# First expert's outputs of the last 1536 tokens by seven block products, and routing rounds spaced wider

## The chip, the core and the metric

One core of one Trainium2 chip. The metric is the device time of one execution in microseconds (us). Engines are named as in the profile: PE does the matmuls, PEld their weight loads, DVE, ACT and POOL are the vector, scalar and GpSimd engines, SP issues DMAs. PSUM has eight banks of 128 x 512 f32; matmuls write there, DVE and ACT read from there, and POOL works in SBUF.

## The reference

An attention with sorted key and value blocks gives x (3072 tokens of 512). What matters here is what follows: a routing matrix from a softmax balanced in eight rounds, and eight experts, each a two-layer network on all tokens, summed with the routing weights.

```
logits = x @ w_gate                       # 3072 x 8
P = np.exp(logits - logits.max())
for _ in range(8):
    P /= P.sum(1, keepdims=True) + 1e-09  # a row step
    P /= P.sum(0, keepdims=True) + 1e-09  # a column step
    P *= N / E
for e in range(8):
    h = np.maximum(x @ w1[e], 0.0)        # 512 -> 1024, the hidden layer
    out += P[:, e:e+1] * (h @ w2[e])      # 1024 -> 512, the output layer
```

## The kernel before

**Tiles.** Tokens are in 24 tiles of 128. xtT holds x transposed (four blocks of 128 features), hT a piece of the hidden layer, transposed, osbl the output sum (acc(t) is the part for tile t), glog the logits and later the routing weights, 24 x 8 per partition in f32.

**Stages.** Up to 106 us the four batches (768 tokens each) go through attention; the first expert's hidden and output layers for batches 0 and 1 are woven in. From 106.7 us on comes the part that changes: a loop of 56 slots (lines 867 to 881). In each slot the first expert does one step for batch 2 or 3 (last_two, line 837): a hidden step (hidden0, line 393) is four matmuls of 384 tokens and a relu on ACT; an output step (output0, line 402) is four matmuls of 512 columns, half of a tile's eight, and after two such steps the tile is copied from PSUM to osbl on ACT (keep, and keep_scaled for batch 3, which multiplies by the routing weight).

**Routing.** balance (line 642) is a generator whose 19 steps are dealt out to named slots. Three find the maximum and exponentiate; then each of eight rounds has a row step (five DVE instructions on glog, lines 668 to 672) and a column step (one matmul with ones on PE that sums over partitions, line 675, then three DVE instructions, 676 to 679). PE's part is kept in program order in all rounds, DVE's in the first five. Rounds end at slot 39.

**Other work in the loop.** From slot 27 on each slot also does a step of the second expert's hidden layer (hidden, line 688). Hidden and output layers of experts 1 to 7 use seven products of half blocks in place of eight (Strassen's scheme in Winograd's form). hidden makes four blocks of 128 x 512 in seven steps of two matmuls each; ACT takes three products to SBUF (lines 717, 721, 726) and one by relu (739), DVE merges three with a custom instruction that adds and clips (712) and subtracts a fourth into h3 (740). It needs sums of x made ahead: sum_x (line 121), four subtractions of 128 x 1024 bf16 on DVE for each 1024 tokens, in slots listed in works. sum_w makes the sums of w1, sum_w2 (line 631) those of w2, eight subtractions on POOL. scale0 (823) multiplies tiles of the first expert by the routing weight on ACT, six of them in the loop, twelve later; gather (744) multiplies later experts' products by their weight and adds them to osbl on DVE.

**Output by seven products.** output7 (line 766) takes a pair of tiles and makes seven products of four matmuls of 256 columns in two PSUM tiles, u and x. u is summed on through five products and read in between, so a product must wait for the read of the one before it in u. The sums of h that it needs are made on POOL by sum_h (755), three instructions for a pair: hs has the sums, h3 the difference that DVE made.

**Who waits where.** Buffers: hT two, h3 two, hs three, the pool bk five PSUM banks (hidden steps and the routing's small matmuls), op three (outputs). Instructions wrapped in pin stay in program order on their engine; the others may be moved by the scheduler that builds the program. At slot 40 a copy on POOL of the finished weights (held, line 880) comes ahead of the second expert's sum_w2 (sums(8)), so that POOL starts this work when routing is done. After the loop, two more hidden steps, and then (line 885) the 21 thirds of experts 1 to 7, each with four pairs of outputs beside the hidden steps of the next third.

Of the kernel before, what the change touches and what calls it, by code (L numbers as in the profile page):

```python
# [13 lines left out]
F32 = mybir.dt.float32  # L14
BF16 = mybir.dt.bfloat16
AF = mybir.ActivationFunctionType
# [9 lines left out]
def kernel(  # L26
# [15 lines left out]
    NT = 24  # L42
# [72 lines left out]
    def acc(t, c=0, n=Dm):  # L115
        return osbl[t // 18][:, t % 18, c:c + n]
# [276 lines left out]
    def hidden0(c0, hTs, hbank, fbs=range(8)):  # L393
        for fb in fbs:
            hps = hbank()
            for kk in range(4):
                pin(nc.tensor.matmul(hps[:, 0:384], w1t[0][:, kk, fb * 128:(fb + 1) * 128],  # L397
                                     xtT[:, kk, c0:c0 + 384], start=(kk == 0), stop=(kk == 3)))
            nc.scalar.activation(out=hTs[:, fb, 0:384], in_=hps[:, 0:384], func=AF.Relu)
            yield  # L400

    def output0(c0, hTs, obank, done, tts=range(3)):
        for tt in tts:
            oacc = obank()
            for fb in range(8):
                pin(nc.tensor.matmul(oacc, hTs[:, fb, tt * 128:(tt + 1) * 128],  # L406
                                     w2t[0][:, fb, :], start=(fb == 0), stop=(fb == 7)))
                if fb == 3:
                    yield
            done(c0 // 128 + tt, oacc)  # L410
            yield
# [1 line left out]
    def keep(t, oacc):  # L413
        (nc.vector.tensor_copy if 6 <= t < 12 else nc.scalar.copy)(acc(t), oacc)

    def keep_scaled(t, oacc):
        nc.scalar.activation(out=acc(t), in_=oacc, func=AF.Copy,
                             scale=glog[:, t, 0:1])

    wct = {}  # L420

    def sum_w(e):
# [123 lines left out]
    with ExitStack() as c2:  # L546
# [61 lines left out]
        for _ in ex:  # L608
# [12 lines left out]
    op = ctx.enter_context(tc.tile_pool(name="op", bufs=3, space=bass.MemoryType.PSUM,  # L621
                                        reuse_waits="tile"))
    osbl[1] = osp.tile([128, 6, Dm], F32, name="osbl1")
    load_w2(1)

    def bank():
        return bk.tile([128, 512], F32, name="bk")

    w2s = {}

    def sum_w2(e):
        w2s[e] = (w2q.tile([128, 4, 4, Dm // 2], BF16, name="w2s") if e % 2 else
                  wcp.tile([128, 4, 4, Dm // 2], BF16, name="w2e"))
        for k in (0, 2):
            b11, b12 = (w2t[e][:, 4 + k:6 + k, d:d + 256] for d in (0, 256))
            b21, b22 = (w2t[e][:, k:k + 2, d:d + 256] for d in (0, 256))
            t1, t2, t3, t4 = (w2s[e][:, j, k:k + 2, :] for j in range(4))
            for a, b, c in ((b12, b11, t1), (b22, t1, t2), (b22, b12, t3), (b21, t2, t4)):
                pin(nc.gpsimd.tensor_tensor(out=c, in0=a, in1=b, op=ALU.subtract))
                yield  # L640
# [100 lines left out]
                                       op0=ALU.max, op1=ALU.subtract)  # L741
        yield

    def gather(e, t, c, ps):
        o = acc(t, c, ps.shape[-1])
        nc.vector.scalar_tensor_tensor(out=o, in0=ps, scalar=glog[:, t, e:e + 1], in1=o,  # L746
                                       op0=ALU.mult, op1=ALU.add)

# [3 lines left out]

    hs = {}

    def sum_h(i, hT, f0=0, f1=4, hold=lambda ins: ins):

        if f0 == 0:
            hs[i] = hsp.tile([128, 3, 4, 128], BF16, name="hs")
        s1, s2, s4 = (hs[i][:, j, f0:f1] for j in range(3))
        a11, a21, a12, a22 = (hT[:, f + f0:f + f1, t + 128 * i:t + 128 * i + 128]  # L760
                              for f in (4, 0) for t in (0, 512))
        for a, b, o, c in ((a21, a22, ALU.add, s1), (s1, a11, ALU.subtract, s2),
                           (a12, s2, ALU.subtract, s4)):
            hold(nc.gpsimd.tensor_tensor(out=c, in0=a, in1=b, op=o))  # L764

    def output7(e, p, i, hT):
        a, b = 8 * p + i, 8 * p + 4 + i
        ha, hb = slice(128 * i, 128 * i + 128), slice(512 + 128 * i, 640 + 128 * i)
        s1, s2, s4 = (hs[i][:, j] for j in range(3))
        s3 = h3[e, p][:, :, ha]  # L770
        t1, t2, t3, t4 = (w2s[e][:, j] for j in range(4))
        obank = lambda: op.tile([128, Dm], F32, name="oacc")
        last = e == E - 1 and p == 2
        u = (bank if last and i % 2 else obank)()[:, 0:256]
        x = (bank if last and i else obank)()
        x0, x1 = x[:, 0:256], x[:, 256:512]
        b11, b21, b22 = w2t[e][:, 4:8, 0:256], w2t[e][:, 0:4, 0:256], w2t[e][:, 0:4, 256:512]

        def add(ps, h, w, first):
            for fb in range(4):  # L780
                nc.tensor.matmul(ps, h[:, fb, :], w[:, fb, :], start=(first and fb == 0),  # L781
                                 stop=(fb == 3), skip_group_check=True)

        def upper():
            add(u, hT[:, 4:8, ha], b11, True)
            gather(e, a, 0, u)

        def lower():
            add(x0, hT[:, 0:4, ha], b21, True)

        for one in (lower, upper) if a == 0 and e == 1 else (upper, lower):
            one()
            yield
        add(u, s2, t2, False)
        gather(e, a, 256, u)
        yield
        add(x1, s1, t1, False)
        gather(e, b, 256, x1)
        yield
        add(u, s3, t3, False)  # L800
        gather(e, b, 256, u)
        yield
        add(x1, s4, b22, False)
        gather(e, a, 0, x)
        store(e, a)
        yield
        add(u, hT[:, 0:4, hb], t4, False)
        gather(e, b, 0, u)
        store(e, b)
        yield  # L810

# [18 lines left out]
    def sums(n):  # L830
        while n and queue:
            if next(queue[0], 0) is None:
                n -= 1
            else:
                queue.pop(0)

    def last_two():
        for bb, done in ((2, keep), (3, keep_scaled)):
            hT = htp.tile([128, 8, 1024], BF16, name="hT")
            halves = [(bb * S + c, hT[:, :, c:c + 384]) for c in (0, 384)]  # L840
            for c0, hTs in halves:
                yield from hidden0(c0, hTs, bank)
            for c0, hTs in halves:
                yield from output0(c0, hTs, lambda: op.tile([128, Dm], F32, name="oacc"), done)

    hTs, AHEAD = {}, 5

# [12 lines left out]
            next(old)  # L860
            yield

    tail0, chain, ahead = last_two(), balance(), hiddens()
    x1, x2 = sum_x(1), sum_x(2)
    works = {12: x0, 18: x1, 22: x1, 25: x1, 26: x1, 41: x2, 43: x2, 46: x2, 48: x2}
    scaled = {41: 0, 42: 4, 43: 1, 45: 5, 47: 2, 49: 6}
    for n in range(56):
        next(tail0)
        if n >= 27:
            next(ahead)  # L870
            if n == 50:
                sum_h(0, hTs[0], 0, 3)
        if n in works:
            next(works[n], 0)
        if n in scaled:
            scale0([scaled[n]])
        if n in (0, 2, 4, 6, 9, 11, 14, 16, 19, 21, 23, 25, 27, 29, 31, 33, 35, 37, 39):
            next(chain)
        if n == 40:
            pin(nc.gpsimd.tensor_copy(held, glog[0:96, NT - 1, 0:2]))  # L880
            sums(8)

    for _ in range(28 + AHEAD - 2 - 29):
        next(ahead)
    for n in range(1, 3 * (E - 1) + 1):
        e, p, hT = 1 + (n - 1) // 3, (n - 1) % 3, hTs[n - 1]
        d = 2 + n // 3
        fetch = n == 1 or n % 3 == 0 and d < E
        if fetch:
            load_w1(d)  # L890
            queue.append(sum_w(d))
        for i in range(4):
            if e == 1:
                scale0([t for t in (8 * p + i, 8 * p + 4 + i)
                        if t < 18 and t not in scaled.values()])
            end = n == 3 * (E - 1)
            hold = pin if end else lambda ins: ins
            if i == 0:
                sum_h(0, hT, 3, hold=hold)
            if i < 3 - end:  # L900
                sum_h(i + 1, hT, 3 if end and i == 0 else 0, hold=hold)
            elif i == 3 and not end:
                sum_h(0, hTs[n], 0, 3)
                if n == 3 * (E - 1) - 1:
                    sum_h(1, hTs[n], 0, 3)
            sums(1 + i // 2)
            for _ in (output8 if end and i == 3 else output7)(e, p, i, hT):
                next(ahead, 0)
        if fetch:
            load_w2(d)  # L910
            queue.append(sum_w2(d))
# [30 lines left out]
```

## Time and profile before

| | us |
|---|---|
| median of 3 runs | 667.71 (667.61 to 667.75) |
| the profiled execution | 667.97 |
| its span, first to last instruction | 666.2 |
| the loop of 56 slots and two hidden steps, on PE | 106.7 to 163.8 |
| DVE busy, 118 to 130 us | 9.69 of 12.00 |
| DVE busy, 130 to 140 us | 7.98 of 10.00 |
| POOL busy, 106.8 to 140 us | 0 |
| POOL busy, 140 to 150 us | 5.99 of 10.00 |
| ACT busy, 130 to 140 us | 7.56 of 10.00 |

PE's granted clock is 0.999 of full speed. Read the table as one stage: PE has work all the time (no gap worth a line), ACT and DVE are three quarters busy, POOL stands idle until the routing rounds are through and works after that. In a line of a timeline the first number is the start in us, the second the duration, then engine, line, operation, output <- inputs, shapes, and in brackets the idle time before it with what ended it. Durations of one engine's neighbours overlap a little; the distance between starts is what an instruction takes of its engine.

### The profile page before, as it was taken

The page shows a single profiled execution, that of the slowest core. Times are in us where ns is not written, and L with a number is a line of the kernel's source. Part 1 is how long each engine was busy: PE and PEld are TensorE (multiplying, and loading weights), DVE is VectorE, ACT ScalarE, POOL GpSimd, SP SyncE. Part 2 cuts the span into 40 slices and gives each one's busy share as a digit, 9 for nine tenths or more (in the row PEclk, how much of TensorE's full clock was granted, in tenths as well). Part 3 has the DMA queues.
Part 4 walks back from the last instruction along what each step waited for, and adds up shares of the span by engine and source line. Part 5 has one row for each costly group of instructions (what it writes and reads, how often), then busy time and mean ns, then how long its engine had stood idle before and what let it go on. Part 6 is the DMA issues. An engine that isn't in the chain of part 4 may idle for free.

```text
span 666.2 us, 13218 instructions
## 1 busy us (share of the span) xinstructions
PE 658.0 (99%) x5141; PEld 435.5 (65%) x5141; DVE 557.9 (84%) x1128; ACT 300.3 (45%) x535; POOL 471.0 (71%) x500
## 2 busy tenths in 40 slices
PE   7999999999999999999999999999999999999997
PEld 3766675554666666666666666666666666666666
DVE  6656876785888898998989898988998989898996
ACT  5775773476455443333334333433343334333430
POOL 4813353037897998898897999689886999646652
PEclk9999999999999999999999999999999999999999
DMA  9998964003041240033103040034003130001124
GB/s 188 172 220 143 150 110 64 1 1 63 1 64 16 49 64 1 0 64 44 21 1 64 1 64 2 1 63 64 1 1 65 16 50 1 1 0 62 68 95 159
DMA packets 33375, 36.96 MB, mean 55 GB/s; under 512 B 2112, under 2 KB 26400, under 8 KB 33312
## 3 DMA queue, kind: packets, MB, share of 16 engines
q0 software_dynamic: 26784, 27.03, 25.9%
q1 hardware_dynamic: 6416, 8.99, 4.3%
q8 instruction: 40, 0.66, 0.4%
q14 instruction: 23, 0.19, 0.1%
q10 hardware_dynamic: 112, 0.10, 0.1%
HBM read 52.45 MB, written 6.29 MB: 88 GB/s over the span
## 4 chain that ended last, share of the span: by engine, by line
PE 95%; DVE 2%; DMA 1%; ACT 0%; issue 0%; POOL 0%; ACTq 0%; DVEq 0%; POOLq 0%
PE bk L694 38%; PE oacc L781 38%; PE bk L397 3%; PE bank L406 3%; PE oacc L406 3%; PE bank L397 2%; PE bank L244 1%; PE pair L365 1%; PE bank L204 1%; PE bank L226 1%; PE bk L781 1%; PE bank L255 1%; DMA vsb<-vs 1%; PE bk L817 1%; DVE vs L283 0%; PE bank L190 0%
## 5 line engine op out<-in xcount | busy, mean ns | idle before, releaser
L746 DVE SCALAR_TENSOR_TENSOR osbl<-oacc,glog,osbl 128x256 f32<-128x256 f32 (+1 forms) x490 | 255.7, 524 | 27.9 <-PE oacc L781 18.2
L764 POOL TENSOR_TENSOR hs<-hT 128x512 bf16<-128x512 bf16 (+2 forms) x105 | 98.6, 951 | 72.3 <-DVE hT L712 72.2
L694 PE MATMUL bk<-xtT,w1e 128*128 128x512 bf16 x504 | 148.6, 379 | 0.0
L712 DVE CUSTOM_DVE_ANT_0 hT<-bk,p 128x512 bf16<-128x512 f32 x168 | 116.1, 691 | 26.7 <-PE bk L694 23.5
L781 PEld LDWEIGHTS <-hT 128*128 128x128 bf16 x996 | 97.4, 98 | 62.6 <-issue 0.2
L781 PEld LDWEIGHTS <-hs 128*128 128x128 bf16 x996 | 97.4, 98 | 61.2 <-issue 1.6
L781 PE MATMUL oacc<-w2e,hT 128*128 128x256 bf16 x796 | 119.7, 273 | 0.0
L717 ACT COPY p<-bk 128x512 f32<-128x512 f32 x84 | 49.3, 587 | 147.4 <-PE bk L694 147.0
L764 POOL TENSOR_TENSOR hs<-hs,hT 128x512 bf16<-128x512 bf16 (+2 forms) x105 | 99.6, 958 | 4.5 <-ACT hT L739 0.2
L764 POOL TENSOR_TENSOR hs<-hT,hs 128x512 bf16<-128x512 bf16 (+2 forms) x105 | 99.1, 952 | 4.7
L694 PE MATMUL bk<-xc,wc 128*128 128x512 bf16 x336 | 99.8, 379 | 0.0
L739 ACT ACTIVATE hT<-bk 128x512 bf16<-128x512 f32 x84 | 50.2, 597 | 96.1 <-PE bk L694 96.1
L781 PE MATMUL oacc<-w2e,hs 128*128 128x256 bf16 x612 | 91.8, 273 | 0.0
L694 PEld LDWEIGHTS <-w1e 128*128 128x128 bf16 x672 | 65.7, 98 | 12.1
L740 DVE SCALAR_TENSOR_TENSOR h<-bk,hT 128x512 bf16<-128x512 f32 x84 | 57.2, 681 | 3.9 <-ACT hT L739 3.9
L712 DVE CUSTOM_DVE_ANT_0 hT<-bk,u 128x512 bf16<-128x512 f32 x84 | 58.0, 690 | 2.5 <-PE bk L694 2.5
L721 ACT COPY u<-bk 128x512 f32<-128x512 f32 x84 | 49.2, 586 | 23.8 <-PE bk L694 23.2
L726 ACT COPY p<-bk 128x512 f32<-128x512 f32 x84 | 49.3, 587 | 23.4 <-PE bk L694 23.4
L694 PEld LDWEIGHTS <-wc 128*128 128x128 bf16 x504 | 49.3, 98 | 8.0 <-issue 0.2
L781 PE MATMUL oacc<-w2s,hs 128*128 128x256 bf16 x364 | 53.3, 272 | 0.0
L694 PE MATMUL bk<-xtT,wc 128*128 128x512 bf16 x168 | 50.0, 379 | 0.0
L694 PE MATMUL bk<-xc,w1e 128*128 128x512 bf16 x168 | 50.0, 379 | 0.0
(149 smaller groups left out, 791.4 us busy)
## 6 DMA issues: line engine op xcount, KB each, us to landing
w1e<-in_moe_w_dram POOLq DMA_DIRECT2D x7, 1024.0 KB, 8.1
w2e<-in_moe_w_dram POOLq DMA_DIRECT2D x7, 1024.0 KB, 8.9
out_dram<-osbl SPq DMA_DIRECT2D x23, 256.0 KB, 2.0
kvq<-in_v_dram POOLq DMA_DIRECT2D x3, 768.0 KB, 10.6
kvq<-in_k_dram POOLq DMA_DIRECT2D x3, 768.0 KB, 11.5
vsb<-vs SPq DMA_DIRECT2D x18, 97.5 KB, 4.6
kvq<-in_q_dram POOLq DMA_DIRECT2D x4, 384.0 KB, 10.2
kvq<-in_q_dram POOLq DMA_DIRECT2D x2, 768.0 KB, 20.2
```

What stands on the lines that cost most here:

```text
L397: pin(nc.tensor.matmul(hps[:, 0:384], w1t[0][:, kk, fb * 128:(fb + 1) * 128], xtT[:, kk, c0:c0 + 384], start=(kk == 0), stop=(kk == 3)))
L406: pin(nc.tensor.matmul(oacc, hTs[:, fb, tt * 128:(tt + 1) * 128], w2t[0][:, fb, :], start=(fb == 0), stop=(fb == 7)))
L694: hold(nc.tensor.matmul(ps, wa[:, kk, :], xa[:, kk, :], start=(first and kk == 0), stop=(kk == 1), skip_group_check=True))
L712: nc.vector._custom_dve(TENSOR_ADD_SAT, out=out, in0=ps, in1=other, s0=TOP, s1=0.0)
L717: still(nc.scalar.copy(p1, u))
L721: still(nc.scalar.copy(u2, u))
L726: still(nc.scalar.copy(p5, v))
L739: still(nc.scalar.activation(out=c21, in_=u, func=AF.Relu))
L740: nc.vector.scalar_tensor_tensor(out=h3[e, p][:, i, :], in0=u, scalar=0.0, in1=c22, op0=ALU.max, op1=ALU.subtract)
L746: nc.vector.scalar_tensor_tensor(out=o, in0=ps, scalar=glog[:, t, e:e + 1], in1=o, op0=ALU.mult, op1=ALU.add)
L764: hold(nc.gpsimd.tensor_tensor(out=c, in0=a, in1=b, op=o))
L781: nc.tensor.matmul(ps, h[:, fb, :], w[:, fb, :], start=(first and fb == 0), stop=(fb == 3), skip_group_check=True)
```

## The change

Batch boundaries are dropped for tokens 1536 to 3071. They are taken as a part "s" of 512 tokens (tiles 12 to 15) and a part of 1024 (tiles 16 to 23). Hidden layers are plain products, 512 tokens wide (hidden_plain). Outputs go through output7 with the first expert's sums of w2, in two pairs for "s" and four for the other part. As the weights aren't ready, gather doesn't multiply for this expert: a first product of a block is copied to osbl on ACT, a later one added on DVE. All 24 tiles are then scaled by scale0 (six in the loop as before, 18 in the second expert's outputs). sum_w2(0) runs on POOL at slot 0, in a buffer of the pool that holds w2; sum_h for the six pairs runs on POOL in slots 8, 9, 34, 37, 44 and 51; for "s" POOL also makes h3, for the other part DVE does. The loop has 66 slots: 8 hidden steps of "s" (called a), 16 of the other part (b), 14 output steps (c) and 28 (d), in the order of the string below. The next expert's hidden steps start at slot 37, the rounds' steps are at wider distances and end at slot 56, and the copy that holds POOL back is gone, with sum_w2(1) done in two halves at slots 40 and 48.

```diff
-    def keep_scaled(t, oacc):
-        nc.scalar.activation(out=acc(t), in_=oacc, func=AF.Copy,
-                             scale=glog[:, t, 0:1])
...
+    w2s = {0: wq.tile([128, 4, 4, Dm // 2], BF16, name="w2e")}
     load_w2(1)
...
-    def gather(e, t, c, ps):
+    def gather(e, t, c, ps, first=False):
         o = acc(t, c, ps.shape[-1])
+        if e == 0:
+            if first:
+                nc.scalar.copy(o, ps)
+            else:
+                nc.vector.tensor_tensor(out=o, in0=ps, in1=o, op=ALU.add)
+            return
...
+    def hidden_plain(p, c0, half):
+        hT = h0[p] = htp.tile([128, 8, 1024], BF16, name="hT")
+        h3[0, p] = h3p.tile([128, 4, 512], BF16, name="h3")
+        for f in range(8):
+            for c in ((half, 0) if half == 512 else (0,)):
+                ps = bank()
+                for kk in range(4):
+                    pin(nc.tensor.matmul(ps, w1t[0][:, kk, f * 128:(f + 1) * 128],
+                                         xtT[:, kk, c0 + c:c0 + c + 512],
+                                         start=(kk == 0), stop=(kk == 3)))
+                nc.scalar.activation(out=hT[:, f, c:c + 512], in_=ps, func=AF.Relu)
+                if f > 3 and c == 0 and half == 512:
+                    nc.vector.scalar_tensor_tensor(
+                        out=h3[0, p][:, f - 4], in0=ps, scalar=0.0, in1=hT[:, f, 512:1024],
+                        op0=ALU.max, op1=ALU.subtract)
+                yield
...
+    def rest_of_first():
+        a, b = hidden_plain("s", 2 * S, 256), hidden_plain(2, 2 * S + 512, 512)
+        c, d = outputs_of("s", 12, 256), outputs_of(2, 16, 512)
+        for x in "a" * 8 + "b" * 6 + "cbcbcbccbcbcbccbcbcbbccc" + "d" * 28:
+            next({"a": a, "b": b, "c": c, "d": d}[x])
+            yield
...
-    works = {12: x0, 18: x1, 22: x1, 25: x1, 26: x1, 41: x2, 43: x2, 46: x2, 48: x2}
-    scaled = {41: 0, 42: 4, 43: 1, 45: 5, 47: 2, 49: 6}
-    for n in range(56):
-        next(tail0)
-        if n >= 27:
+    works = {12: x0, 14: x1, 22: x1, 30: x1, 37: x1, 43: x2, 49: x2, 55: x2, 60: x2}
+    scaled = {57: 0, 58: 4, 60: 1, 61: 5, 63: 2, 64: 6}
+    for n in range(66):
+        next(first)
+        if n >= 37:
             next(ahead)
-            if n == 50:
-                sum_h(0, hTs[0], 0, 3)
+        if n == 0:
+            for _ in sum_w2(0):
+                pass
+        if n in (8, 9):
+            sum_h(n - 8, h0["s"], hold=pin, half=256)
+            if n == 8:
+                pin(nc.gpsimd.tensor_tensor(
+                    out=h3[0, "s"][:, :, 0:256], in0=h0["s"][:, 4:8, 0:256],
+                    in1=h0["s"][:, 4:8, 256:512], op=ALU.subtract))
+        if n in (34, 37, 44, 51):
+            sum_h((34, 37, 44, 51).index(n), h0[2], hold=pin)
+        if n == 60:
+            sum_h(0, hTs[0], 0, 3)
...
-        if n in (0, 2, 4, 6, 9, 11, 14, 16, 19, 21, 23, 25, 27, 29, 31, 33, 35, 37, 39):
+        if n in (0, 2, 4, 6, 9, 11, 15, 18, 23, 26, 31, 34, 38, 40, 44, 46, 50, 52, 56):
             next(chain)
-        if n == 40:
-            pin(nc.gpsimd.tensor_copy(held, glog[0:96, NT - 1, 0:2]))
-            sums(8)
+        if n in (40, 48):
+            sums(4)
```

output7 and sum_h take the distance of a pair's tiles as a parameter (half: 256 or 512 tokens), and output7's matmuls are pinned for the first expert.

More of the change, by code (lines that the diff above doesn't have):

```diff
@@ L627, in bank @@
         return bk.tile([128, 512], F32, name="bk")
-    w2s = {}
     def sum_w2(e):
-        w2s[e] = (w2q.tile([128, 4, 4, Dm // 2], BF16, name="w2s") if e % 2 else
-                  wcp.tile([128, 4, 4, Dm // 2], BF16, name="w2e"))
+        if e:
+            w2s[e] = (w2q.tile([128, 4, 4, Dm // 2], BF16, name="w2s") if e % 2 else
+                      wcp.tile([128, 4, 4, Dm // 2], BF16, name="w2e"))
         for k in (0, 2):
@@ L753, with sum_h @@
     hs = {}
-    def sum_h(i, hT, f0=0, f1=4, hold=lambda ins: ins):
+    def sum_h(i, hT, f0=0, f1=4, hold=lambda ins: ins, half=512):
         if f0 == 0:
@@ L760, in sum_h @@
         a11, a21, a12, a22 = (hT[:, f + f0:f + f1, t + 128 * i:t + 128 * i + 128]
-                              for f in (4, 0) for t in (0, 512))
+                              for f in (4, 0) for t in (0, half))
         for a, b, o, c in ((a21, a22, ALU.add, s1), (s1, a11, ALU.subtract, s2),
@@ L764, in sum_h, with output7 @@
             hold(nc.gpsimd.tensor_tensor(out=c, in0=a, in1=b, op=o))
-    def output7(e, p, i, hT):
-        a, b = 8 * p + i, 8 * p + 4 + i
-        ha, hb = slice(128 * i, 128 * i + 128), slice(512 + 128 * i, 640 + 128 * i)
+    def output7(e, p, i, hT, t0=None, half=512):
+        a = (8 * p if t0 is None else t0) + i
+        b = a + half // 128
+        ha, hb = slice(128 * i, 128 * i + 128), slice(half + 128 * i, half + 128 * i + 128)
+        hold = pin if e == 0 else lambda ins: ins
         s1, s2, s4 = (hs[i][:, j] for j in range(3))
@@ L780, in add @@
             for fb in range(4):
-                nc.tensor.matmul(ps, h[:, fb, :], w[:, fb, :], start=(first and fb == 0),
-                                 stop=(fb == 3), skip_group_check=True)
+                hold(nc.tensor.matmul(ps, h[:, fb, :], w[:, fb, :], start=(first and fb == 0),
+                                      stop=(fb == 3), skip_group_check=True))
         def upper():
             add(u, hT[:, 4:8, ha], b11, True)
-            gather(e, a, 0, u)
+            gather(e, a, 0, u, True)
         def lower():
@@ L794, in output7 @@
         add(u, s2, t2, False)
-        gather(e, a, 256, u)
+        gather(e, a, 256, u, True)
         yield
         add(x1, s1, t1, False)
-        gather(e, b, 256, x1)
+        gather(e, b, 256, x1, True)
         yield
@@ L807, in output7 @@
         add(u, hT[:, 0:4, hb], t4, False)
-        gather(e, b, 0, u)
+        gather(e, b, 0, u, True)
         store(e, b)
@@ L835, in sums, with outputs_of @@
                 queue.pop(0)
[L837 to L844, printed above, removed]
+    h0 = {}
+    def hidden_plain(p, c0, half):
[14 more added lines that the diff above has]
+                yield
+    def outputs_of(p, t0, half):
+        for i in range(half // 128):
+            yield from output7(0, p, i, h0[p], t0, half)
+    def rest_of_first():
[4 more added lines that the diff above has]
+            yield
     hTs, AHEAD = {}, 5
@@ L861, in hiddens @@
             yield
-    tail0, chain, ahead = last_two(), balance(), hiddens()
+    first, chain, ahead = rest_of_first(), balance(), hiddens()
     x1, x2 = sum_x(1), sum_x(2)
-    works = {12: x0, 18: x1, 22: x1, 25: x1, 26: x1, 41: x2, 43: x2, 46: x2, 48: x2}
-    scaled = {41: 0, 42: 4, 43: 1, 45: 5, 47: 2, 49: 6}
-    for n in range(56):
-        next(tail0)
-        if n >= 27:
-            next(ahead)
-            if n == 50:
-                sum_h(0, hTs[0], 0, 3)
+    works = {12: x0, 14: x1, 22: x1, 30: x1, 37: x1, 43: x2, 49: x2, 55: x2, 60: x2}
[3 more added lines that the diff above has]
+        if n >= 37:
+            next(ahead)
+        if n == 0:
[11 more added lines that the diff above has]
+            sum_h(0, hTs[0], 0, 3)
         if n in works:
@@ L894 @@
                 scale0([t for t in (8 * p + i, 8 * p + 4 + i)
-                        if t < 18 and t not in scaled.values()])
+                        if t not in scaled.values()])
             end = n == 3 * (E - 1)
```

## The prediction

> **What bounds the kernel now.** I read the page's busy times first, then the chain that ended last, then the timelines of PE, DVE and POOL over the part that changes, from 106.7 us (the first expert's tokens 1536 on) to 163.8 us (the second expert's first output).
>
> ```profile
> PE 658.0 (99%) x5141; PEld 435.5 (65%) x5141; DVE 557.9 (84%) x1128; ACT 300.3 (45%) x535; POOL 471.0 (71%) x500
> PE 95%; DVE 2%; DMA 1%; ACT 0%; issue 0%; POOL 0%; ACTq 0%; DVEq 0%; POOLq 0%
> ```
>
> PE is busy in 99% of the span and is 95% of the chain. So a microsecond of matmul taken out is a microsecond won, as long as nothing makes PE wait; DVE, at 84%, is the next to become the limit. From the timeline of PE:
>
> ```profile
> 130.57 0.81 PE L397 MATMUL bk<-xtT,w1e 128*128 128x384 bf16 x4
> 131.22 0.59 PE L694 MATMUL bk<-xc,wc 128*128 128x512 bf16 x2
> ...
> 147.37 1.03 PE L406 MATMUL oacc<-w2e,hT 128*128 128x512 bf16 x4
> 148.24 0.59 PE L694 MATMUL bk<-xtT,w1e 128*128 128x512 bf16 x2
> ...
> 163.78 0.60 PE L781 MATMUL oacc<-w2e,hT 128*128 128x256 bf16 x4
> 164.21 0.59 PE L694 MATMUL bk<-xtT,w1e 128*128 128x512 bf16 x2
> ```
>
> The distance from one start to the next is what a step costs: four products of 384 columns 0.65 us, four of 512 columns 0.87 us, four of 256 columns 0.43 us. A 256-wide product costs half of a 512-wide one; the weight loads (0.098 us each) stay hidden.
>
> **PE.** The x·w1 products of the twelve tiles are 32 steps of 0.65 = 20.8 us now and 24 steps of 0.865 = 20.8 us after: nothing won. The outputs are 24 steps of 0.865 = 20.8 us now; after, six pairs of seven products are 42 steps of 0.433 = 18.2 us. So PE is asked for **2.6 us less**. The 31 hidden steps of the next expert that are laid between (0.433 each) and the ten small matmuls of the routing stay.
>
> **DVE.** This is where the change pays. One routing round on DVE, from its timeline (starts are what counts):
>
> ```profile
> 121.95 0.17 DVE L676 TENSOR_SCALAR cs<-bk 128x8 f32<-128x8 f32 x1 [0.98 <-PE bk L675]
> 122.16 0.20 DVE L678 RECIPROCAL cs<-cs 128x8 f32<-128x8 f32 x1
> 122.39 0.36 DVE L679 TENSOR_TENSOR glog<-glog,cs 128x192 f32<-128x192 f32 x1
> 122.79 0.35 DVE L668 TENSOR_REDUCE rs<-glog 128x24 f32<-128x192 f32 x1
> 123.17 0.18 DVE L669 TENSOR_SCALAR rs<-rs 128x24 f32<-128x24 f32 x1
> 123.39 0.30 DVE L670 RECIPROCAL rs<-rs 128x24 f32<-128x24 f32 x1
> 123.72 0.36 DVE L671 TENSOR_TENSOR glog<-glog,rs 128x192 f32<-128x192 f32 x1
> 124.11 0.50 DVE L672 TENSOR_REDUCE cs<-glog 128x8 f32<-128x192 f32 x1
> 124.53 0.68 DVE L128 TENSOR_TENSOR xc<-xtT,xc 128x1024 bf16<-128x1024 bf16 x1
> ```
>
> A column step is 0.84 us (121.95 to 122.79), a row step 1.74 us (to 124.53). Before, DVE had little else to do while the rounds ran: the twelve tiles left PSUM through ACT, and only the late rounds met the next expert's evictions. After, the seven products put two sums per pair on DVE (256 and 512 wide), and tokens 2048 to 3071 four subtractions for h3; and the rounds now run to slot 56 of 66, beside 20 hidden steps, not to slot 39 beside 13.
>
> I add up the second half, from the column matmul at slot 31 to the end of the phase. PE needs there, for the first expert, six slots to 37 (four of 0.433, two of 0.865) and 28 of 0.433, then 31 hidden steps of 0.433 (29 in slots 37 to 65, two after) and four column matmuls of 0.14: 1.7 + 1.7 + 12.1 + 13.4 + 0.6 = **29.6 us** with rounding. DVE is asked for: five column and four row steps, 4.2 + 7.0; the 16 evictions and subtractions that belong to 31 hidden steps, at 0.61 from start to start, 9.8; two last subtractions for h3, 1.2; the sums of five pairs, 5.3 (they read PSUM and one tile of SBUF as the gathers do: 0.39 to 0.48 for 256 columns, 0.66 to 0.75 for 512, taken at 0.40 + 0.66); five steps of sum_x at 0.60, 3.0. Together **30.5 us, before any waiting**. DVE is full, and PE waits for it in three places: at a column matmul whose row step isn't done; at an eviction that keeps a bank; and, new, in each pair at the seventh product, which must not touch its bank before DVE has added the fifth's sum to SBUF, about 1.3 us earlier (0.4 us in the pair that ends at slot 37, right behind the row step of slot 34).
>
> **The waits on POOL.** Before, the copy at line 880 holds POOL back until routing is done, and then:
>
> ```profile
> 146.65 1.48 DVE L128 TENSOR_TENSOR xc<-xtT 128x1024 bf16<-128x1024 bf16 x1
> 148.16 1.53 DVE L128 TENSOR_TENSOR xc<-xtT,xc 128x1024 bf16<-128x1024 bf16 x1
> ...
> 150.87 1.60 DVE L128 TENSOR_TENSOR xc<-xtT,xc 128x1024 bf16<-128x1024 bf16 x1
> ```
> ```profile
> 143.93 0.18 POOL L880 CAST held<-glog 96x2 bf16<-96x2 f32 x1 [37.69 <-PE bk L397]
> ...
> 146.41 1.16 POOL L639 TENSOR_TENSOR w2s<-w2e 128x512 bf16<-128x512 bf16 x1
> 147.53 1.61 POOL L639 TENSOR_TENSOR w2s<-w2e,w2s 128x512 bf16<-128x512 bf16 x1
> ```
>
> The same sum_x step takes 0.68 us at 124.53, with POOL idle, and 1.48 to 1.60 us with POOL at work: it ends as the POOL instruction in front of it ends, plus its own time, and POOL's instruction at 147.53 is 0.45 us longer. The evictions of line 712 (PSUM and one SBUF tile) stay at 0.69 in both. So an SBUF + SBUF TENSOR_TENSOR on DVE and a TENSOR_TENSOR on POOL take turns. The change takes the hold away and gives POOL 8 + 18 + 1 more instructions in this phase: sum_w2(0) at its start, then in the second half 12 of sum_h, 8 of sum_w2(1), 3 smaller: 20 × 1.13 + 3 × 0.95 = 25.5 us, and some 4.5 us of being held up itself. It works about three quarters of the second half.
>
> What a wait costs: five sum_x steps, 0.85 each (mean of 1.48, 1.53, 1.60 less 0.69) = 4.2. The nine routing multiplies (lines 671, 679) are SBUF + SBUF too, but no row shows one beside a busy POOL. Ends: nothing (like line 712), or the whole of a POOL instruction, 1.13. I take half of one, 0.57, what a random arrival finds, because sum_x is the nearest row in kind: 5.1. Together 9.3, times three quarters, 7.0 us. [...]
>
> DVE then needs 30.5 + 7.0 = 37.5 us against PE's 29.6: 7.9 us late. The last eviction and sum (1.3) need not be done when the phase ends. In the first half two sum_x steps (slots 12 and 14) come before a column step and beside sum_w2(0): between 0 and 1.2 us at the column matmul of slot 23; I take 0.6. PE and DVE also wait in turns: a column step starts 0.3 us after its matmul, five times, half of it filled: 0.8. Stalls 7.9 - 1.3 + 0.6 + 0.8 = **8.0 us**, less 2.6: **+5.4 us**.
>
> **What costs nothing.** ACT gets 24 copies of 256 columns for 12 evictions of 512, and six more scalings of 0.72. In a pair with hidden steps (6.1 us) that is 4 × 0.59 and four copies of between 0.3 and 0.59 us: under 5 us. In the last nine slots the scalings fill ACT; without that room a copy would be late by one scaling, 0.7 us. sum_h of the fourth pair needs POOL by slot 61; by POOL's own sum it is there about when PE, not delayed, would come, up to 3 us late with the turns taken; DVE's lateness covers that. The load of expert 2's w1 queues on POOL behind sum_h: between 0 and 1 us, taken as 0, for POOL idles 1.8 us at 178.6. Expert 1's w2 takes the other buffer of its pool, the first is free again long before it is loaded. After the phase, PE is back to back to the end, so the difference stays.
>
> The profiled execution is 667.97 us (span 666.2 and 1.8 around it): 667.97 + 5.4 = 673.4, and the median of the three runs lies 0.26 lower: **673.1 us**.
>
> **Rivals.** About 0.2% (1.3 us) is what a measurement of this kernel can tell from no change.
> - *The multiplies don't wait* (chance 0.22). For: no row shows them waiting. Only sum_x does: DVE 30.5 + 4.2 × 3/4 = 33.7, 4.1 us late, stalls 4.1 - 1.3 = 2.8 without the two small terms and 4.2 with them; where the seventh products' waits come in bursts, 6. Less 2.6, and off the median: 667.9 to 671.1, half of that within 0.2%.
> - *More forms wait* (0.12). If the single-input instructions of a row step (lines 669, 670) take turns with POOL as well, each row step loses another 0.6 to 1.1 us, in six rounds and at three quarters: 2.7 to 5 us more, 675.8 to 678. [...]
> - *Faster* (0.11): DVE's shortage without waits is only 30.5 - 29.6 = 0.9 us. If POOL is through with its work between the rounds' multiplies (it idles until the hidden layer is there) and the two sums of a pair fit between the row steps, PE waits 0.9 us and the change wins 1.7: 666.0. It decides at 2.6 us of stalls. Against it: POOL's 25.5 us fall into the same 29.6.
>
> The forecast has 0.55, 671.1 to 675.8. Range: 667.3 to 677.5; it leaves out the faster case and the far end of the longest waits. Faster 0.11, same 0.11, slower 0.78.
>
> **What would show it.** In the changed profile: four 256-wide products still 0.43 us apart; lines 671 and 679 (by new numbers) with means above 0.36 us, up to 0.9; sum_x at 1.3 to 1.6; gaps of PE of 0.5 to 2 us ahead of seventh products and of column matmuls, between slots 18 and 61, with DVE named as the releaser; DVE over 95% busy from about 131 us to the end of the phase. The phase would then end some 5 us later than 163.8. If PE has gaps under 2.6 us in all, the prediction is wrong; if the multiplies stay at 0.36, the size is.

## The result and the profile after

The changed kernel takes 675.78 us (median of 4 executions, 675.66 to 676.79) against 667.73 us before (667.61 to 667.82): ratio 1.0124, 95% interval 1.0106 to 1.0142. It is slower by 8.05 us; the forecast was 5.4 us slower, with a time of 673.1 us. The profiled execution is the longest of the four, 676.79 us, with a span of 675.0 us.

The page's busy times and the chain's shares by engine, of the changed kernel:

```profile
PE 659.8 (98%) x5181; PEld 439.9 (65%) x5181; DVE 573.9 (85%) x1144; ACT 302.6 (45%) x545; POOL 503.6 (75%) x526
PE 90%; DVE 6%; ACT 2%; DMA 1%; issue 1%; POOL 0%; ACTq 0%; SPq 0%; DVEq 0%
```

PE's share of the chain fell from 95% to 90% and DVE's rose from 2% to 6%: the kernel now waits for DVE for part of the time. The phase itself, from the first product of these tokens to the second expert's third output step (its first sums of h), was 106.68 to 165.98 us before and is 106.25 to 174.88 us now: 59.30 us became 68.63 us, 9.3 us more. So the whole loss lies inside it. The timeline of PE in the changed kernel (start, duration, what it is, and in brackets the idle time and its releaser):

```profile
125.30 0.60 PE L785 MATMUL oacc<-w2e,hs 128*128 128x256 bf16 x4
127.75 0.39 PE L671 MATMUL bk<-cs,onesc 128*128 128x8 f32 x2 [1.85 <-DVE cs L668]
...
138.75 0.59 PE L690 MATMUL bk<-xc,wc 128*128 128x512 bf16 x2 [0.24 <-ACT p L713]
141.94 0.60 PE L671 MATMUL bk<-cs,onesc 128*128 128x8 f32 x2 [2.59 <-DVE cs L668]
142.39 1.01 PE L785 MATMUL oacc<-w2e,hT 128*128 128x256 bf16 x4
143.19 1.06 PE L690 MATMUL bk<-xc,wc 128*128 128x512 bf16 x2
...
156.96 0.60 PE L785 MATMUL oacc<-w2e,hT 128*128 128x256 bf16 x4 [0.54 <-DVE osbl L746]
157.39 0.59 PE L690 MATMUL bk<-xc,w1e 128*128 128x512 bf16 x2
```

In these lines L671 is the column matmul of a routing round, L668 the last instruction of the row step that it needs, L785 an output product, L690 a hidden step and L746 the addition of a product to the output sum. The difference of two starts, less the time of the step between them, is what PE lost: 125.30 to 127.75 is 2.45 us for a step of 0.43, so 2.02 us lost ahead of the column matmul of slot 23. Summed in this way over the phase, PE lost 0.3 us before and 12.0 us after: 2.6 in the first half (up to the column matmul of slot 31), 2.76 ahead of the fifth round's column matmul at 141.94, 3.6 in nine smaller gaps of the second half, and 3.1 in a kind of its own: from 142 us on the steps are 0.85 us apart where they should be 0.43. The windows view says why (columns: stretch, length, then busy us of PE, PEld, DVE, ACT and POOL, then the granted clock, the DMA share and GB/s):

```profile
142.00:148.00 6.00, 6.00 (x23) 3.47 (x24) 4.78 (x10) 1.33 (x3) 5.84 (x6) 0.50 0.00 1
148.00:152.00 4.00, 4.00 (x31) 2.82 (x30) 3.61 (x8) 2.27 (x5) 3.84 (x4) 1.00 0.00 0
```

The granted clock of TensorE was 0.50 for 6.8 us, from 141.15 us, still inside the longest wait, to 147.98. A PE that is 6.00 of 6.00 busy is not a PE at full speed.

The timeline of DVE shows what made it late, and that of POOL what stood beside it:

```profile
120.52 2.08 DVE L128 TENSOR_TENSOR xtT<-xtT 128x1024 bf16<-128x1024 bf16 x1
...
136.57 0.42 DVE L746 TENSOR_TENSOR osbl<-oacc,osbl 128x256 f32<-128x256 f32 x1 [1.15 <-PE oacc L785]
...
143.01 0.80 DVE L675 TENSOR_TENSOR glog<-glog,cs 128x192 f32<-128x192 f32 x1
...
144.23 0.62 DVE L665 TENSOR_SCALAR rs<-rs 128x24 f32<-128x24 f32 x1
144.89 0.30 DVE L666 RECIPROCAL rs<-rs 128x24 f32<-128x24 f32 x1
145.23 1.04 DVE L667 TENSOR_TENSOR glog<-glog,rs 128x192 f32<-128x192 f32 x1
```
```profile
119.82 2.23 POOL L902 TENSOR_TENSOR h<-hT 128x1024 bf16<-128x1024 bf16 x1
...
143.55 1.27 POOL L635 TENSOR_TENSOR w2s<-w2e 128x512 bf16<-128x512 bf16 x1
```

Alone, the same DVE instructions took 0.36 (multiplies, L675 and L667), 0.18 (the addition of 1e-9, L665), 0.30 (the reciprocal) and 0.68 us (sum_x, L128), as the lines of before show. Beside POOL the multiplies take up to 1.14 (mostly 0.80 to 1.04), the addition mostly 0.62 and once 1.16, sum_x up to 2.08; the reciprocal stays as it was. The line at 136.57 is another loss: DVE stood idle for 1.15 us at an addition that waited for PE, with the row step of round 5 queued behind it, which had been ready at 135.42. Its last instruction began at 141.38, and PE waited for that at 141.94.

### The profile page after: what moved, and what is told of

Its sections match the earlier page's. It is cut to its first block, busy times and chain, and to the rows that moved or that the text cites. A ratio compares the mean times of both kernels' runs of the same rounds, so it can differ in the third digit from the quotient of the medians.

```text
span 675.0 us, 13357 instructions
## 1 busy us (share of the span) xinstructions
PE 659.8 (98%) x5181; PEld 439.9 (65%) x5181; DVE 573.9 (85%) x1144; ACT 302.6 (45%) x545; POOL 503.6 (75%) x526
## 4 chain that ended last, share of the span: by engine, by line
PE 90%; DVE 6%; ACT 2%; DMA 1%; issue 1%; POOL 0%; ACTq 0%; SPq 0%; DVEq 0%
PE oacc L785 38%; PE bk L690 36%; PE bank L406 3%; PE bank L397 2%; PE bk L850 2%; PE bank L244 1%; PE pair L365 1%; PE bank L204 1%; PE bank L226 1%; DMA osbl<-in_k_dram 1%; PE bk L785 1%; PE bank L255 1%; DVE glog L667 1%; DVE rs L665 1%; PE bk L821 1%
## 5 line engine op out<-in xcount | busy, mean ns | idle before, releaser
L766 POOL TENSOR_TENSOR hs<-hT 128x512 bf16<-128x512 bf16 (+2 forms) x111 | 106.8, 974 | 85.9 <-DVE hT L708 76.4
L690 PE MATMUL bk<-xtT,w1e 128*128 128x512 bf16 x504 | 149.1, 381 | 0.0
L785 PEld LDWEIGHTS <-hT 128*128 128x128 bf16 x1068 | 104.8, 98 | 67.4 <-issue 1.7
L785 PEld LDWEIGHTS <-hs 128*128 128x128 bf16 x1068 | 104.8, 98 | 66.2 <-issue 2.8
L785 PE MATMUL oacc<-w2e,hT 128*128 128x256 bf16 x868 | 130.8, 273 | 0.9 <-DVE osbl L746 0.8
L766 POOL TENSOR_TENSOR hs<-hs,hT 128x512 bf16<-128x512 bf16 (+2 forms) x111 | 106.7, 970 | 5.0 <-ACT hT L735 0.2
L766 POOL TENSOR_TENSOR hs<-hT,hs 128x512 bf16<-128x512 bf16 (+2 forms) x111 | 106.2, 964 | 5.2
L785 PE MATMUL oacc<-w2e,hs 128*128 128x256 bf16 x684 | 103.5, 274 | 0.0
L690 PE MATMUL bk<-xc,wc 128*128 128x512 bf16 x336 | 100.4, 381 | 0.2 <-ACT p L713 0.2
L690 PEld LDWEIGHTS <-w1e 128*128 128x128 bf16 x672 | 66.0, 98 | 10.2
L690 PEld LDWEIGHTS <-wc 128*128 128x128 bf16 x504 | 49.4, 98 | 6.4 <-issue 0.4
L785 PE MATMUL oacc<-w2s,hs 128*128 128x256 bf16 x364 | 53.1, 272 | 0.1
L785 PEld LDWEIGHTS <-h 128*128 128x128 bf16 x356 | 35.0, 98 | 23.3 <-issue 1.1
L690 PE MATMUL bk<-xc,w1e 128*128 128x512 bf16 x168 | 50.0, 379 | 0.0
```

The source lines that it names most:

```text
L690: hold(nc.tensor.matmul(ps, wa[:, kk, :], xa[:, kk, :], start=(first and kk == 0), stop=(kk == 1), skip_group_check=True))
L785: hold(nc.tensor.matmul(ps, h[:, fb, :], w[:, fb, :], start=(first and fb == 0), stop=(fb == 3), skip_group_check=True))
```

## The experiments

My theory after the result: DVE is late because its SBUF + SBUF instructions, and the additions of 1e-9, take turns with POOL. The rivals: the order of work on DVE (too much between column matmuls, whatever POOL does), and the lost clock.

**Operands in PSUM.** If turns on SBUF are the cause, the same instructions with one operand in PSUM don't wait, as the evictions of before, from PSUM and one SBUF tile, stay at 0.69 us beside a busy POOL.

```diff
-        rs2 = mpc.tile([128, NT], F32)
-        cs1 = mpc.tile([128, E], F32)
...
+            one = bank()
+            csps, rs2, cs1 = one[:, 0:128], one[:, 128:128 + NT], one[:, 256:256 + E]
-            csps = bank()[:, 0:128]
```

> The changed kernel with the row sums and the scaled column sums of every routing round kept in PSUM instead of SBUF, so that the multiplies, the additions of 1e-9 and the reciprocals read one SBUF tile at most; nothing else is changed. Theory of turns (DVE waits because these instructions and POOL's take turns): in the changed kernel the eight row multiplies, eight column multiplies and eight additions take 3.3 + 1.9 + 3.2 = 8.4 us more than they do beside an idle POOL; here they are back at 0.36 to 0.45 and about 0.2 us, the gap of PE ahead of the fifth column matmul shrinks below 1.5 us, its clock stays full, and the time falls by 5 to 8 us, to 668 to 671 us. Theory of load (DVE has too much work in any case, and its order makes it late): the multiplies may get shorter but the time falls by under 2.5 us, above 673 us.

Measured: 671.48 us (median of 10), ratio to before 1.0058 (1.0038 to 1.0078), 4.3 us less than the changed kernel. The eight row multiplies and eight additions by source line, first of the changed kernel and then of this one (least, median and greatest in ns, first and last start):

```profile
L667 DVE TENSOR_TENSOR glog<-glog,rs x8: 357/1006/1040, 113.1 to 161.5; 128x192 f32<-128x192 f32 x8
L665 DVE TENSOR_SCALAR rs<-rs x8: 179/628/1160, 112.6 to 160.5; 128x24 f32<-128x24 f32 x8
```
```profile
L667 DVE TENSOR_TENSOR glog<-glog,bk x8: 337/354/354, 113.3 to 155.2; 128x192 f32<-128x192 f32 x8
L665 DVE TENSOR_SCALAR bk<-bk x8: 180/191/192, 112.7 to 154.7; 128x24 f32<-128x24 f32 x8
```

The waits are gone to the last one, with POOL as busy as it was (9.69 us of the 10 from 140 to 150 us, in both). About half of the loss came back with them. The phase still takes 62.42 us, with gaps of 6.2 us. PE's timeline at the fifth round's column matmul:

```profile
139.31 0.39 PE L670 MATMUL bk<-cs,onesc 128*128 128x8 f32 x2 [1.90 <-DVE cs L668]
```

That gap is 1.90 us, where under 1.5 was expected. The clock stays at 1.00 in this execution and in four others (670.58 to 671.37 us); in the other five it is 0.989 or 0.997, and they take 671.59 us or more, so the median lies just over the 668 to 671 us that were expected. Turns of the rounds' own instructions with POOL are shown to be about half of the loss, the largest single part; the order of the work and the sum_x steps (up to 2.64 us) are left.

**The hold put back.** The changed kernel with POOL's sum_w2(1) behind the routing again, as before.

```diff
-        if n in (40, 48):
-            sums(4)
+        if n == 56:
+            pin(nc.gpsimd.tensor_copy(held, glog[0:96, NT - 1, 0:2]))
+            sums(8)
```

> The changed kernel with the hold on POOL put back: the eight sums of the second expert's w2 wait for the finished routing weights (one copy on POOL at slot 56), as before the change; POOL keeps sum_w2(0) and sum_h beside the rounds. Theory of turns: POOL is free of eight of its 20 instructions in rounds six to eight, whose waits (rows 0.67 and 0.45, columns 0.05 to 0.5 us) go by half; 1 to 2 us faster, 674 to 675 us; the gap ahead of the fifth column matmul (2.8 us) stays, as sum_h causes it. Theory of load: no change within 0.5 us. A third way: POOL, now later with the fourth pair's sums or with the second expert's, makes PE wait, and the time rises by up to 3 us.

Measured: 681.67 us, ratio 1.0200 (1.0165 to 1.0235), 5.9 us more than the changed kernel: the third way, and about twice its 3 us. The phase becomes 2.9 us shorter (65.76 us), though not all through POOL: 0.56 of it are at the column matmul of slot 23, ahead of the edit (1.46 us lost there, not 2.02), and 1.6 because the clock was at 0.50 for 3.4 us and not 6.8. What follows pays for it. POOL and then PE:

```profile
162.83 0.96 POOL L766 TENSOR_TENSOR hs<-hT 128x384 bf16<-128x384 bf16 x1 [11.69 <-DVE hT L708]
...
163.87 1.60 POOL L635 TENSOR_TENSOR w2s<-w2e 128x512 bf16<-128x512 bf16 x1
```
```profile
177.72 1.25 PE L785 MATMUL oacc<-w2s,hs 128*128 128x256 bf16 x5 [4.61 <-POOL hs L766]
```

POOL idled for 11.69 us, had eight sums of w2 ahead of it at 163.87, and PE stood 4.77 us at 177.72 for sums of h. The hold can't simply be kept: the rounds now end too late for it.

**Filling the gap.** Six matmuls that nobody reads in the 2.76 us gap, so that PE isn't idle there, to see whether it then keeps its clock.

```diff
...
+            if it == 4:
+                for _ in range(6):
+                    tc.keep_in_program_order(nc.tensor.matmul(
+                        csps, w1t[0][:, 0, 0:128], xtT[:, 0, 0:512], start=True, stop=True))
...
```

> The changed kernel with six more matmuls of 512 columns, whose result nobody reads, laid on PE just ahead of the fifth round's column matmul (1.3 us of added work in a gap of 2.8 us). If the low granted clock from about 142 to 148 us follows from that gap, the clock stays full, the seven steps after it take 0.43 us instead of 0.8, and the time falls by 2 to 3 us, to 673 to 674 us, though PE does more. If the clock drops for another reason, nothing changes within 0.5 us, or the time rises by up to 1.3 us.

Measured: 677.83 us (675.72 to 680.14), ratio 1.0135 (1.0086 to 1.0184): no gain. In its profiled execution the phase begins 4.15 us later than in the changed kernel's, from a loss ahead of it, where nothing is edited (the mean granted clock is 0.992 over the whole execution and 1.00 in every stretch from 106.2 to 180 us); so the phases are to be compared, 67.23 us here and 68.63 us in the changed kernel, or the two executions that kept a clock of 1.000, 675.72 and 676.17 us, with the changed kernel's own at 1.000, 675.66 us. In the phase the clock did stay at 1.00, but PE's timeline shows new gaps:

```profile
145.31 0.39 PE L676 MATMUL bk<-cs,onesc 128*128 128x8 f32 x2 [1.30 <-DVE cs L668]
...
151.83 0.60 PE L790 MATMUL oacc<-w2e,hT 128*128 128x256 bf16 x4 [1.78 <-DVE osbl L751]
```

1.94 us are lost ahead of a seventh product at 151.83, and 1.35 at the eighth column matmul. While PE ran at half clock, DVE caught up; a PE at full clock waits for it a little later instead. So the 3.1 us of slow steps were worth 1.4 us at most, the difference of the two phases (0.56 us of it lie at slot 23 again, ahead of the edit).

**The hold taken out of the kernel before.** All else as before: POOL beside the rounds, and none of the change's own load on DVE.

```diff
-        if n == 40:
-            pin(nc.gpsimd.tensor_copy(held, glog[0:96, NT - 1, 0:2]))
+        if n == 16:
             sums(8)
```

> The kernel before the change with one edit: the hold on POOL is taken out and the eight sums of the second expert's w2 start at slot 16, beside rounds three to five. No seven products, no additions on DVE, the old spacing. Theory of turns: beside these 9 us of POOL work the row and column multiplies go from 0.36 to about 1.0 us and the additions from 0.18 to about 0.6, PE waits up to 1 us at each of two or three column matmuls: 1.5 to 3 us slower than before, 669 to 671 us. Theory of load: the multiplies stay at 0.36 us and the time at 667.7 us.

Measured: 670.12 us, ratio 1.0033 (1.0020 to 1.0045), 2.5 us slower. DVE's row multiply beside POOL (after it, at 126.45, it takes 0.36):

```profile
116.42 1.04 DVE L671 TENSOR_TENSOR glog<-glog,rs 128x192 f32<-128x192 f32 x1
```

POOL was busy from 114.8 to 125.3 us; the three column matmuls of that time, at 118.13, 123.37 and 127.39, came 0.86, 0.91 and 0.34 us late, 2.1 of the 2.5 us. The turns are there without any of the seven products.

**The same with operands in PSUM.** The edit of the first experiment made in the fourth.

> The kernel before the change with the hold on POOL taken out and sum_w2(1) at slot 16, as in e4_before_pool (670.1 us, multiplies 0.88 to 1.04 us), and with the rounds' operands in PSUM. Theory of turns: the multiplies and additions are back at 0.36 and 0.19 us beside the working POOL, and the 2.5 us that e4_before_pool lost come back: 667.5 to 668.3 us. If POOL's work slows the rounds in another way, the time stays at 669.5 to 670.5 us.

Measured: 669.05 us, ratio 1.0028 (1.0017 to 1.0039). The multiplies are back at 0.35 and the additions at 0.19, and the column matmuls beside POOL aren't late any more, but only 1.1 of the 2.5 us came back. Four gaps of 0.31 us stand ahead of hidden steps, with no releaser in the trace. The edit keeps one of the five banks of bk from the row step to the column step, so a hidden step may wait for a bank; that is argued, not shown. The expectation was missed by 0.8 us.

**The rounds earlier.** The order on DVE was the remaining suspect. The rounds' slots are moved so that they end at slot 48, sum_x and scale0 with them, once with the operands in PSUM and once in SBUF.

```diff
-    works = {12: x0, 14: x1, 22: x1, 30: x1, 37: x1, 43: x2, 49: x2, 55: x2, 60: x2}
-    scaled = {57: 0, 58: 4, 60: 1, 61: 5, 63: 2, 64: 6}
+    works = {0: x0, 1: x1, 3: x1, 9: x1, 27: x1, 50: x2, 54: x2, 58: x2, 62: x2}
+    scaled = {50: 0, 52: 4, 54: 1, 56: 5, 59: 2, 62: 6}
...
-        if n in (0, 2, 4, 6, 9, 11, 15, 18, 23, 26, 31, 34, 38, 40, 44, 46, 50, 52, 56):
+        if n in (0, 2, 4, 6, 9, 10, 13, 14, 18, 19, 23, 24, 30, 31, 36, 38, 42, 43, 48):
```

> The changed kernel with the row sums and scaled column sums in PSUM as in e1_psum, and with DVE's other work moved out of its full stretch: the routing rounds end at slot 48 instead of 56 (five of them by slot 30), the sums of x for tokens 0 to 2047 are made in slots 0 to 9 and 27, those for tokens 2048 on in slots 50 to 62, after the rounds, and scale0 runs from slot 50. Theory of DVE's work (turns and load together make DVE late, and PE waits for it): the stalls fall from about 9 us to under 2 us, and the seven products' 2.6 us come out: 665 to 667 us, faster than both kernels. Rival (the seven products can't pay, since each pair's two additions on DVE hold up the seventh product whatever the order): stalls stay above 3 us, 668 us or more.

> The same new order as in e5_early_psum, but with the rounds' operands in SBUF as in the changed kernel. Theory of turns: the rounds in slots 6 to 30 meet sum_w2(0) and the first sum_h on POOL, each row step 1.1 us and each column step 0.5 us longer; PE waits at several column matmuls before slot 23, and the time lies 2 to 5 us above e5_early_psum, at 668 to 671 us. If the order alone was at fault, it is within 1 us of e5_early_psum.

Measured: 668.80 us with PSUM, ratio 1.0024 (1.0012 to 1.0035), and 674.09 us with SBUF, ratio 1.0093 (1.0080 to 1.0107). In the new order the PSUM operands are worth 5.3 us, in the old one 4.3; the order alone is worth 1.7 us (675.78 to 674.09), and 2.7 with PSUM (671.48 to 668.80). Both causes are real, and the turns with POOL are the larger here. The version with PSUM missed its expectation of 665 to 667 us: 3.8 us of gaps are left: 1.27 are of the edit's own making, for the first sum_x, moved to the start, and the copy behind it on DVE for the first routing matmul met sum_w2(0) on POOL (1.56 and 1.03 us, for 0.68 and 0.16 alone); 0.74 and 0.72 are at seventh products behind a sum_x. The version with SBUF lies above its 668 to 671 us as well, 5.3 us and not 2 to 5 over the other.

**The sum_x steps moved, in three steps.** First to slots 3, 5, 7, 25, 29, 51, 52, 58 and 59, with that copy on ACT:

> As e5_early_psum, with its three remaining gaps of PE taken on: the sums of x for tokens 0 to 2047 come after the first two small matmuls of the routing and in slots where POOL idles (3, 5, 7, 25, 29), the identity for the first of these matmuls is copied by ACT instead of DVE (there it waited for POOL, 1.03 us), and the sums for tokens 2048 on come right behind a pair's additions (slots 51, 52, 58, 59), not ahead of them. Theory of DVE's work: the gap of 1.3 us ahead of the first small matmul and the two of 0.7 us ahead of seventh products go, under 1.2 us of stalls are left, and the time is 668.8 - 2.7 = 666.1 us, 665.5 to 666.7, faster than before the change. Rival (DVE's load, not its order, sets these gaps): other gaps take their place, 667.5 us or more.

Measured: 667.31 us, ratio 0.9996 (0.9974 to 1.0018), the same time as before the change; the expected 666.1 wasn't reached. Gaps of 2.76 us are left, 1.12 and 0.38 of them at seventh products behind two sum_x in a row. Then the late steps of x2 at slots 51, 58 and 65, and the fourth in the second expert's outputs:

> As e8_late_x2, with the sums of x for tokens 2048 on spread one to a pair: right behind a pair's additions in slots 51, 58 and 65, and the fourth in the second expert's outputs. In e8_late_x2 two of them in a row make the next pair's first addition late, and PE waits 1.12 and 0.38 us ahead of two seventh products; its other gaps are 1.3 us. Theory of DVE's work: one sum_x fits between two pairs' additions, both gaps go, and the time falls by 1.3 to 1.6 us, to 665.7 to 666.0 us, 1.7 us under the kernel before (2.6 us of products less some 1.2 us of stalls). Rival (what is left is the price of seven products, each pair's two additions): the gaps stay and the time with them, 667.0 to 667.4 us.

Measured: 668.08 us, ratio 1.0004 (0.9986 to 1.0022), so this one missed. Those two gaps went, but the sum_x of slot 65 is the first line here, from DVE's timeline, and the second is PE's:

```profile
162.55 3.98 DVE L128 TENSOR_TENSOR xc<-xtT,xc 128x1024 bf16<-128x1024 bf16 x1
```
```profile
167.57 1.03 PE L784 MATMUL oacc<-w2s,hs 128*128 128x256 bf16 x8 [3.27 <-DVE osbl L747]
```

3.98 us for an instruction of 0.68, while POOL ran short sums of h (128 columns each) one behind the other from 161.84 to 165.94; PE stood 3.42 us. Last, two steps of x2 in the second expert's outputs and the rounds' slots 23 to 38 one later:

> As e9_one_x2, where the gaps of the phase went down to 1.1 us but one sum_x, laid at slot 65 beside five short POOL instructions in a row, took 3.98 us and cost PE 3.4 us. Here the third and fourth sums of x for tokens 2048 on both lie in the second expert's outputs, behind its first two pairs' start, where POOL's instructions are the long ones; the column steps at slots 23 and 36 come one slot later. Theory of DVE's work: the 3.4 us go, two gaps of up to 0.4 us may come in the second expert's outputs, and the time is 668.0 - 3.4 + 0.4 - 0.5, 664.5 to 665.7 us, 2 to 3 us under the kernel before. Rival (some sum_x always meets POOL somewhere, and what is saved in one place is lost in another): 667 us or more.

Measured: 666.98 us against 667.60 for the kernel before in the same runs, ratio 0.9986 (0.9975 to 0.9997). It is faster than both kernels, by 0.6 us and so less than expected (664.5 to 665.7). The phase takes 58.35 us. PE's largest gap in it:

```profile
135.55 0.60 PE L784 MATMUL oacc<-w2e,hT 128*128 128x256 bf16 x4 [1.17 <-DVE osbl L745]
```

The pair's first addition stood behind a whole row step on DVE: 1.34 of the 1.73 us that PE loses in the phase. The phase is 0.95 us shorter than before the change, so even here more than half of the 2.6 us won on PE is given back.

## Why the prediction was right on the direction and short on the size

**PE's 2.6 us less** held: 256-wide products are still 0.43 us apart (156.96 to 157.39), and the phase's balance closes with it: 12.0 us of lost time, less 0.3 before, less 2.6, is 9.1 of the 9.3 us.

**DVE as the bound** held in kind: column matmuls and seventh products are where PE waits, with DVE as the releaser, as forecast. But DVE was not full. It was busy for 11.16 of 12 us from 119 to 131 us and 9.79 of 10 from 150 to 160, but for 7.62 of 9 from 131 to 140, 8.21 of 10 from 140 to 150 and 9.94 of 12 from 160 to 172, where the prediction has over 95% from 131 us on. PE can wait for a DVE that has time left, when DVE itself waits for PE in between (1.15 us at 136.57).

**Turns with POOL** held, and they are shown by the kernels with operands in PSUM and by the kernel before without its hold. But the terms came out otherwise. After slot 31 the multiplies lost 2.6 us (3.8 in the sum, where half a POOL instruction for each was my estimate); the additions of 1e-9, which I had at nothing, lost 2.3; and the five sum_x only 0.3 (3.2): together 5.2 where the sum has 7.0. Why sum_x lost so little is seen in the timelines of DVE and of POOL:

```profile
139.45 0.68 DVE L128 TENSOR_TENSOR xtT<-xtT 128x1024 bf16<-128x1024 bf16 x1
```
```profile
139.46 1.68 POOL L766 TENSOR_TENSOR hs<-hT 128x512 bf16<-128x512 bf16 x1
```

In these lines whoever starts first goes on. sum_x began just as POOL's instruction of 138.34 (1.15 us) ended, ahead of the next, and it was POOL that took 0.53 us longer; it is the same at 150.43, 156.83 and 166.78, where the POOL instructions that start right behind take 1.48, 1.61 and 1.36 us. I had charged each sum_x with a turn lost. The rival "more forms wait" therefore came true in half: the TENSOR_SCALAR waits (mostly 0.62 us for 0.18, which no row of before showed), the RECIPROCAL does not (0.29 to 0.30 in every round). The measured time lies at that rival's near end (675.8) and at the far end of my own forecast's.

**The step that failed is the first half: "between 0 and 1.2 us at the column matmul of slot 23; I take 0.6".** The mechanism was as written, sum_x and the rounds beside POOL, but the size was 2.6 us, 2.02 of it at that very matmul (1.46 there with the hold back and with the gap filled, whose edits come later). I had counted two sum_x steps there and none of the rest. In the first half DVE lost 6.8 us to POOL: multiplies 2.7, sum_x 2.3, additions 0.9 and the copy of the identity for the first routing matmul 0.9. I charged the multiplies with turns in the second half alone, though POOL makes sum_w2(0), sum_h and h3 in the first.

**Two things were in no term.** One is the order on DVE: at 136.57 an addition that waited for PE held DVE for 1.15 us with the next row step, ready, behind it, and that row step was what the longest gap waited for. The other is the half clock that began in that gap: 3.1 us of slow steps in the profiled execution. By the kernel with the filled gap it costs far less than that: an execution of the changed kernel with a clock of 1.000 takes 675.66 us, 7.9 more than before. At full clock, then, PE's stalls are 7.9 + 2.6 = 10.5 us where I had 8.0. Of the 2.5 missing, 2.0 are the first half (2.6 for 0.6). The second half comes to 7.9 for 7.4, and that is luck in part: with the 5.2 us of turns that were measured in place of 7.0, the same sum gives 30.5 + 5.2 - 29.6 - 1.3 + 0.8 = 5.6. The other 2.3 us have no term in it. The order on DVE, worth 1.7 us in all by the experiment with earlier rounds, is the part of them that is shown; how the rest divides is open.

**What costs nothing** held for ACT, which released PE once in a gap of 0.40 us (138.75), and for POOL: in the phase it is never the releaser of a wait worth a line. The *faster* rival needed POOL's work to fall between the multiplies. It didn't; but the last experiment shows that a version with PSUM operands and another order does come out under the kernel before, by 0.6 us.

## What to carry to other kernels

Before work is taken from the engine that bounds, add up the next engine's work in that very stretch, and price every one of its instructions by its row beside the busy neighbour that the change will give it, small ones and the first half too. And ask whether that engine will stand idle behind the one it serves, with ready work queued: a sum of busy times doesn't show it. Where DVE must work beside POOL on small operands, put one of them in PSUM: here that was worth 4.3 and 5.3 us, and 1.1 of the 2.5 us that POOL beside the rounds cost the kernel before. And a gap that is filled isn't a gap won while the engine behind it is still late.

## What the runs showed of the hardware that was not expected

- A TENSOR_SCALAR of 24 f32 elements per partition on one SBUF tile takes 0.18 us alone and mostly 0.62 (once 1.16) beside a TENSOR_TENSOR on POOL; in PSUM 0.18 to 0.19 in all eight rounds, as the first experiment shows. The RECIPROCAL of the same 24 elements in SBUF takes 0.29 to 0.30 in both.
- The sum_x of slot 65 did not get its turn when POOL's current instruction ended: it took 3.98 us, for 0.68 alone, while POOL ran several short instructions. Why is open.
- The granted clock fell to 0.50 around PE gaps of 2.76 us (the changed kernel, from 141.15 to 147.98 us), 2.75 us (with the hold, for 3.4 us of the stretch from 140 to 150) and 4.77 us (with the hold, 0.50 from 177 to 180 us). It stayed at 1.00 around gaps of 2.02 us (the changed kernel again), 2.41 (the rounds earlier, with the operands in SBUF) and 3.42 (the sum_x of slot 65). So the length of a gap alone does not decide. What else does was not tried by an experiment, and is open.
